# Moving the PSUM copies of the shift-filter gradient from VectorE to ScalarE

## The chip, the cores and the metric

The kernel runs on one core of a Trainium2 chip. The metric is the device time of one execution in microseconds (us). Of the kernel before there are three timed runs and one profiled execution, which is a run of its own with its own time. The engines are named as in the profile: PE is TensorE (matmuls and transposes, with PEld for its weight loads), DVE is VectorE, ACT is ScalarE, POOL is GpSimd, and SP is the engine that issues nearly all DMAs here (its issuing instructions are shown as SPq).

## The reference, cut to what matters

The forward pass adds two branches to its input x (2048 rows of 512): a gated long convolution and a gated bilinear layer. Both read xn, the layernorm of x. The reference returns the output and nine gradients for a given grad_out.

```python
k_shift = sum over t of k_pad[:, t:t+S, :] * shift_k[:, ks-1-t]     # ks = 4 taps per channel
kv = k_shift * v
y  = irfft(rfft(kv) * rfft(ssm_k))[:S] + kv * ssm_D                 # long causal convolution
out = x + xn * y + ((xn @ w_gate) * (xn @ w_up)) @ w_down
# outputs: out, then the gradients of q, k, v, shift_k, ssm_k, ssm_D, w_gate, w_up, w_down
```

Two small gradients matter for the change. The gradient of `shift_k` (512 channels, 4 taps) is, for each channel, the sum over the 2048 rows of the gradient of `k_shift` times `k` shifted by 0 to 3 rows. The gradient of `ssm_D` (512 numbers) is the gradient of the convolution's kernel at lag 0, as its product with `kv` is a sum over the same rows.

## The kernel before, in words

The 2048 rows lie as 128 partitions by 16 row groups (`R`). Early stages normalise x, run the bilinear layer forward and backward in chunks of rows (`ffn1`, `yb`), and do the convolutions as a two-step Fourier transform on PE (`g_fwd`, `g_mul`, `g_inv`). The change lies in the last stage, which fills the last 160 us or so of the span. Its spine is `dw` (from line 1046): for each of 11 blocks `fb` of 128 hidden units it runs `down_grad` (tile `pd`, 16 matmuls, gradient of `w_down`) and then the matmuls into `pu` (gradients of `w_gate` and `w_up`). For these the hidden activations must have the row dimension on partitions: blocks 0 to 6 are transposed on PE (`hid_t`, PSUM tile `pt`, copied by ACT into `nath` and `natd`). Blocks 7 to 10 (`TURNED`) come turned by a DMA (`load_t`, tile `natT`, line 817), except for the last chunk of rows, which `last_t` turns on PE (line 829) and ACT copies to an SBUF tile named `nat7` in the code and `nat` in the profile.

`dw` yields some six times for each block. At each yield the loop at the end of the kernel lets side jobs take a step: `inv_y`; `dsk_gram` from count 27 and then at every second count; `inv_dk` from 35 at every third (gradient of `ssm_k`; after its first part `put_dD` sends out the gradient of `ssm_D`); and `ew` from 10 at every third (elementwise work of DVE: `final` and `bwd`, whose results `put_late` sends out one step later).

`dsk_gram` handles 128 channels at a time (`c` from 0 to 3). For two halves of 64 channels, PE multiplies `dks` (64 channels by rows) by four shifted views of `k`, giving 64 x 256 products in PSUM (`pk`), of which only the diagonal of each 64 x 64 block is wanted. DVE multiplies by the identity (line 1091, tile `kd`) and sums (line 1093, `dsk`). After the four groups the sums are cast (`dskb`), turned by PE (`pts`, line 1101), copied by DVE (`dskt`) and sent out (line 1104). `put_dD` does the same with `dDs`, `ptd` and `dDt` (lines 1017 to 1020).

The order of each engine's instructions is laid down when the program is built. A planner takes the work in the order in which it is written, each engine taking the first that is ready by its own estimate; `tc.high_priority(offset=SOON)` counts its instructions as written 300 earlier, and `tc.issue_after` keeps a DMA's issue behind another. On the chip each engine then goes through its list in order. PSUM has three slots of two banks for tiles made by `P2` (`pk`, `pt`, `pu`, `po`, `pq`) and two of one bank for those made by `P1` (`pd`, `pts`, `ptd`). In SBUF the tag `dd` has two slots, shared by `dd` (from `inv_y`), `kd`, `nat7`, `dskt` and the last `og1`. A slot is free when the last reader of its tile is done; for `dskt` that is its outgoing DMA, for `nat7` the last matmul of its block.

The helpers `act` and `dve` (lines 235 and 238) are plain copies, so all copies of an engine carry one line number in the profile.

Of the kernel before, what the change touches and what calls it, by code (L numbers as in the profile page):

```python
# [9 lines left out]
F32 = mybir.dt.float32  # L10
I32 = mybir.dt.int32
ALU = mybir.AluOpType
ACTF = mybir.ActivationFunctionType
AX = mybir.AxisListType
# [7 lines left out]
P = 128  # L22
NC4 = 4
# [3 lines left out]
SOON = 300  # L27
# [163 lines left out]
def kernel(  # L191
# [24 lines left out]
    nc = tc.nc  # L216
# [17 lines left out]
    def act(o, i):  # L234
        nc.scalar.copy(o, i)  # L235

    def dve(o, i):
        nc.vector.tensor_copy(o, i)  # L238
# [13 lines left out]
    def P2(name, shape, dt=F32):  # L252
        return ps2.tile(shape, dt, name=name, tag="p2")

    def P1(name, shape, dt=F32):
        return ps1.tile(shape, dt, name=name, tag="p1")

    ident = const.tile([P, P], BF, name="ident")
# [658 lines left out]
    c2b = ctx.enter_context(tc.tile_pool(name="c2b", bufs=2, side="right", reuse_waits="tile"))  # L917
# [8 lines left out]
    dsk = c2.tile([P, NC4, 4], F32, name="dsk")  # L926
# [62 lines left out]
    def inv_dk():  # L989
        o5t = c2.tile([P, NC4, P, R], BF, name="o5t", tag="o5k")  # L990
        o5 = out_5.rearrange("(c q) s -> c q s", q=P)
        for rq in range(4):
            gk = gks.pop(0)
            if rq == 0:
                gk_last = load_gk_last()
            for b in range(2):
                po = P2("po", [P, 2, 4, P])
                for h in range(2):
                    for i in range(4):
                        for c in range(2):  # L1000
                            nc.tensor.matmul(po[:, h, i, :], lhsT=(gk_last(c, i) if rq == 3 else gk[:, c, i])[:, cs(2 * b + h)], rhs=TB.IW[:, c, :],
                                             start=(c == 0), stop=(c == 1))
                act(o5t[:, 2 * b:2 * b + 2, :, 4 * rq:4 * rq + 4], po[:].rearrange("q h r s -> q h s r"))
                if b == 1 and rq < 2:
                    gks.append(load_gk(2) if rq == 0 else None)
                if rq == 3:
                    for c in (2 * b, 2 * b + 1):
                        nc.sync.dma_start(o5[c], o5t[:, c].rearrange("q s r -> q (s r)"))
                yield
            if rq == 0:  # L1010
                yield from put_dD(o5t)

    def put_dD(o5t):
        act(dDs[:], o5t[:, :, 0, 0])
        yield
        pt = P1("ptd", [P, P], BF)
        nc.tensor.transpose(pt[:NC4, :], dDs[:], ident[:])
        dDt = c2.tile([NC4, P], BF, name="dDt")
        dve(dDt[:], pt[:NC4, :])
        nc.sync.dma_start(out_6.rearrange("(c p) -> c p", p=128), dDt[:])  # L1020

    def down_grad(fb):
# [56 lines left out]
    def dsk_gram():  # L1079
        for c in range(NC4):  # L1080
            pk = P2("pk", [P, 2, D])
            for r in range(R):
                for h in range(2):
                    c0 = c * 128 + 64 * h
                    nc.tensor.matmul(pk[64 * h:64 * h + 64, h, 0:256], lhsT=dks[:, r, c0:c0 + 64],
                                     rhs=KH[0][:, r:r + 4, c0:c0 + 64], start=(r == 0), stop=(r == R - 1))
            kd = c2b.tile([P, 4, 64], F32, name="kd", tag="dd")
            with tc.high_priority(offset=SOON):
                for h in range(2):
                    hs = slice(64 * h, 64 * h + 64)  # L1090
                    nc.vector.tensor_tensor(kd[hs], pk[hs, h, 0:256].rearrange("q (j c) -> q j c", j=4),
                                            ident[hs, hs].unsqueeze(1).to_broadcast((64, 4, 64)), op=ALU.mult)
                nc.vector.tensor_reduce(dsk[:, c, :], kd[:], axis=AX.X, op=ALU.add)
            yield
        dskb = c2.tile([P, 4, NC4], BF, name="dskb")
        nc.vector.tensor_copy(dskb[:], dsk[:].rearrange("q c i -> q i c"))
        for _ in range(2):
            yield
        pt = P1("pts", [P, 4, P], BF)
        for j in range(4):  # L1100
            nc.tensor.transpose(pt[:NC4, j, :], dskb[:, 3 - j, :], ident[:])
        dskt = c2b.tile([NC4, P, 4], BF, name="dskt", tag="dd")
        dve(dskt[:], pt[:NC4].rearrange("c j q -> c q j"))
        nc.sync.dma_start(out_4.rearrange("(c p) j -> c p j", p=128), dskt[:])
        yield

# [88 lines left out]
    def load_dk():  # L1195
        gks.append(load_gk(0))
        gks.append(load_gk(1))
        yield

    sides = [every(seq(inv_y(), load_dk()), 0, 3), every(dsk_gram(), 27, 2), every(inv_dk(), 35, 3), every(ew(), 10, 3)]  # L1200
    for n, _ in enumerate(dw()):
        for sd in sides:
# [36 lines left out]
```

## Time and profile before

| what | us |
|---|---|
| median of three runs (lowest to highest) | 480.83 (479.9 to 481.28) |
| the profiled execution, its own time | 481.82 |
| its span, first to last instruction | 480.0 |
| busy in the span: PE | 464.5 (97%) |
| busy in the span: DVE | 340.5 (71%) |
| busy in the span: ACT | 305.6 (64%) |
| 8 multiplies of line 1091 | 0.422 each (median) |
| 4 sums of line 1093 | 0.414 each (median) |
| copy `dskt` / copy `dDt` on DVE | 0.679 / 0.204 |

The times of a line in the timeline are its start and its length in us from the span's start. "idle before" is time in which the engine did nothing, with what ended it. The granted clock of TensorE was 0.999 on average. In the trace some records of matmuls are missing, so a group of 16 can be shown as 15.

### The profile page before, as it was taken

The page shows a single profiled execution, that of the slowest core. Times are in us where ns is not written, and L with a number is a line of the kernel's source. Part 1 is how long each engine was busy: PE and PEld are TensorE (multiplying, and loading weights), DVE is VectorE, ACT ScalarE, POOL GpSimd, SP SyncE. Part 2 cuts the span into 40 slices and gives each one's busy share as a digit, 9 for nine tenths or more (in the row PEclk, how much of TensorE's full clock was granted, in tenths as well). Part 3 has the DMA queues.
Part 4 walks back from the last instruction along what each step waited for, and adds up shares of the span by engine and source line. Part 5 has one row for each costly group of instructions (what it writes and reads, how often), then busy time and mean ns, then how long its engine had stood idle before and what let it go on. Part 6 is the DMA issues. An engine that isn't in the chain of part 4 may idle for free.

```text
span 480.0 us, 10366 instructions
## 1 busy us (share of the span) xinstructions
PE 464.5 (97%) x4252; PEld 311.6 (65%) x4293; DVE 340.5 (71%) x609; ACT 305.6 (64%) x349; POOL 14.0 (3%) x30
## 2 busy tenths in 40 slices
PE   7999999999999999999999999999999999999996
PEld 6867755547648447447447743576777687677885
DVE  7889989979366567686777877022257899599893
ACT  4957677659568678779779975375576535233141
POOL 8000000000000000000000000110000000000000
PEclk9999999999999999999999999999999999999999
DMA  8999999989998968968978379999899979999858
GB/s 268 374 381 366 310 296 320 315 300 328 318 288 270 277 202 255 285 200 245 298 235 259 118 272 331 388 329 313 312 361 364 371 260 320 318 267 239 252 155 294
DMA packets 111132, 139.85 MB, mean 291 GB/s; under 512 B 38859, under 2 KB 84336, under 8 KB 109550
## 3 DMA queue, kind: packets, MB, share of 16 engines
q1 hardware_dynamic: 109502, 137.85, 89.7%
q10 hardware_dynamic: 1584, 1.36, 1.0%
q8 instruction: 33, 0.54, 0.5%
q14 instruction: 13, 0.11, 0.1%
HBM read 67.08 MB, written 63.41 MB: 272 GB/s over the span
## 4 chain that ended last, share of the span: by engine, by line
PE 67%; DMA 15%; DVE 14%; issue 2%; SPq 2%; ACT 1%; DVEq 0%; ACTq 0%
PE px L555 15%; PE pgu L512 13%; PE pu L1062 8%; PE py L548 7%; PE pdh L518 6%; PE pd L1026 4%; PE ps L584 3%; DMA khC<-in_A_k_dram 3%; PE pg L613 3%; DMA ssk<-in_A_ssm_k_dram 2%; PE pf L370 2%; PE pt L859 2%; DMA vb<-in_A_v_dram 2%; DMA kb<-KS 2%; DMA x_b<-in_A_q_dram 2%
## 5 line engine op out<-in xcount | busy, mean ns | idle before, releaser
L555 PE MATMUL px<-WT,hd 128*128 128x512 bf16 (+1 forms) x340 | 78.6, 379 | 1.6 <-issue 1.4
L1062 PEld LDWEIGHTS <-xnC 128*128 128x128 bf16 x704 | 67.0, 98 | 8.4 <-issue 0.6
L555 PEld LDWEIGHTS <-hd 128*128 128x128 bf16 (+1 forms) x352 | 32.8, 98 | 44.4 <-issue 7.7
L235 ACT CAST gu<-pgu 128x1024 bf16<-128x1024 f32 (+1 forms) x48 | 45.4, 946 | 16.9 <-PE pgu L512 16.7
L235 ACT CAST GO<-pg 128x1024 bf16<-128x1024 f32 x48 | 46.2, 1015 | 13.8 <-issue 7.2
L235 ACT CAST SP<-ps 128x1024 bf16<-128x1024 f32 x47 | 45.5, 1025 | 13.7 <-PE ps L584 11.8
L512 PE MATMUL pgu<-xt,Wu 128*128 128x256 bf16 (+1 forms) x352 | 53.1, 273 | 1.1 <-DVE kn L238 0.6
L600 DVE TENSOR_TENSOR T<-SP 128x2048 bf16<-128x2048 bf16 x24 | 29.3, 1222 | 34.8 <-ACT SP L235 34.7
L512 PE MATMUL pgu<-xt,Wg 128*128 128x256 bf16 (+1 forms) x352 | 52.8, 273 | 0.0
L1062 PE MATMUL pu<-natd,xnC 128*128 128x256 bf16 x448 | 51.2, 273 | 0.0
L518 PE MATMUL pdh<-gt,WdT 128*128 128x256 bf16 (+1 forms) x352 | 46.9, 273 | 0.1
L235 ACT CAST fst<-pf 128x1024 bf16<-128x1024 f32 x44 | 42.7, 1031 | 5.5 <-issue 2.3
L512 PEld LDWEIGHTS <-Wu 128*128 128x128 bf16 (+1 forms) x352 | 33.0, 100 | 15.6 <-issue 10.7
L548 PE MATMUL py<-Wd,hd 128*128 128x512 bf16 (+1 forms) x167 | 40.2, 379 | 0.8 <-issue 0.5
L235 ACT CAST og<-pu 128x1024 bf16<-128x1024 f32 (+1 forms) x11 | 10.9, 993 | 43.7 <-PE pu L1062 28.3
L518 PEld LDWEIGHTS <-WdT 128*128 128x128 bf16 (+1 forms) x352 | 34.9, 100 | 4.8
L512 PEld LDWEIGHTS <-Wg 128*128 128x128 bf16 (+1 forms) x352 | 34.8, 100 | 3.7
L235 ACT COPY natd<-pt 128x2048 bf16<-128x2048 bf16 x14 | 26.2, 1875 | 12.0 <-PE pt L859 12.0
L533 DVE TENSOR_TENSOR hd<-gu,dh 128x1024 bf16<-128x1024 bf16 (+1 forms) x48 | 30.8, 641 | 0.8
L532 DVE TENSOR_TENSOR hd<-gu 128x512 bf16<-128x512 bf16 (+1 forms) x48 | 19.0, 397 | 16.7 <-ACT gu L235 16.7
L548 PEld LDWEIGHTS <-hd 128*128 128x128 bf16 (+1 forms) x176 | 16.5, 98 | 20.8 <-issue 3.1
L600 DVE TENSOR_TENSOR U<-SP 128x2048 bf16<-128x2048 bf16 x24 | 29.2, 1218 | 0.0
(177 smaller groups left out, 687.4 us busy)
## 6 DMA issues: line engine op xcount, KB each, us to landing
HDD<-hd SPq DMA_DIRECT2D x35, 384.0 KB, 4.5
FD<-fst SPq DMA_DIRECT2D x24, 512.0 KB, 4.9
X<-FD SPq DMA_DIRECT2D x24, 512.0 KB, 5.5
GD<-GO SPq DMA_DIRECT2D x24, 512.0 KB, 3.9
g<-GD SPq DMA_DIRECT2D x11, 1024.0 KB, 8.9
hb<-HDD SPq DMA_DIRECT2D x7, 1344.0 KB, 10.2
bb<-BX SPq DMA_DIRECT2D x8, 512.0 KB, 5.5
BX<-bx SPq DMA_DIRECT2D x7, 512.0 KB, 3.9
```

The lines of the kernel that those rows point to most:

```text
L235: nc.scalar.copy(o, i)
L512: nc.tensor.matmul(pgu[:w, i, t, :], lhsT=W[:, c, f0:f0 + w], rhs=xt[:, :, c, :], start=(c == 0), stop=(c == NC4 - 1))
L518: nc.tensor.matmul(pdh[:w, i, :], lhsT=WdT[:, c, f0:f0 + w], rhs=gt[:, :, c, :], start=(c == 0), stop=(c == NC4 - 1))
L532: nc.vector.tensor_tensor(hd[:fw, fb0:fb0 + n, 0, :], gu[:fw, :n, 0, :], gu[:fw, :n, 1, :], op=ALU.mult)
L533: nc.vector.tensor_tensor(hd[:fw, fb0:fb0 + n, 1:3, :], gu[:fw, :n], dh[:fw, :n].unsqueeze(2).to_broadcast((fw, n, 2, 256)), op=ALU.mult)
L548: nc.tensor.matmul(py[:], lhsT=hd[:fw, fb, 0, ss], rhs=Wd[:fw, fb, :], start=(fb == 0), stop=(fb == NFB - 1))
L555: nc.tensor.matmul(px[:], lhsT=hd[:fw, fb, t, ss], rhs=W[:fw, fb, :], start=(t == 1 and fb == 0), stop=(t == 2 and fb == NFB - 1))
L584: nc.tensor.matmul(ps[32 * q:32 * q + 32, a, :], lhsT=TB.EF[64 * a:64 * a + 64, 4 * g + q, ri].rearrange("p k j -> p (k j)"), rhs=X[64 * a ...
L600: tt(W[:].rearrange("p c a d -> p c (a d)"), A[:, i:i + 1].rearrange("p c a d -> p c (a d)").to_broadcast((P, 2, 2 * D)), B[:].rearrange(" ...
L613: nc.tensor.matmul(pg[q // 2][64 * a:64 * a + 64, q % 2, :], lhsT=TB.EI[32 * q:32 * q + 32, 2 * g + a, yi].rearrange("p k c -> p (k c)"), ...
L1026: nc.tensor.matmul(pd[:fw, :], lhsT=nat_h(fb, r), rhs=goC[:, r, :], start=(r == 0), stop=(r == R - 1))
L1062: nc.tensor.matmul(pu[:, c, :, :fw], lhsT=xnC[:, r, cs(c)], rhs=nat_d(fb, r), start=(r == 0), stop=(r == R - 1))
```

## The change

The eight multiplies no longer read PSUM. ACT copies each half of `pk` as float32 into `kd` in SBUF, and DVE multiplies there in place and sums. One `kd` tile of twice the size now serves two of the four groups, so that the four groups take two tiles of tag `dd` in place of four. The copies, multiplies and sums have no raised priority. The wait between `dskb` and the transposes into `pts` is four yields in place of two (the transposes are written at count 43 in place of 39). The copies `dskt` and `dDt` are made by ACT.

```diff
         dDt = c2.tile([NC4, P], BF, name="dDt")
-        dve(dDt[:], pt[:NC4, :])
+        act(dDt[:], pt[:NC4, :])
         nc.sync.dma_start(out_6.rearrange("(c p) -> c p", p=128), dDt[:])
...
-            kd = c2b.tile([P, 4, 64], F32, name="kd", tag="dd")
-            with tc.high_priority(offset=SOON):
-                for h in range(2):
-                    hs = slice(64 * h, 64 * h + 64)
-                    nc.vector.tensor_tensor(kd[hs], pk[hs, h, 0:256].rearrange("q (j c) -> q j c", j=4),
-                                            ident[hs, hs].unsqueeze(1).to_broadcast((64, 4, 64)), op=ALU.mult)
-                nc.vector.tensor_reduce(dsk[:, c, :], kd[:], axis=AX.X, op=ALU.add)
+            if c % 2 == 0:
+                kd = c2b.tile([P, 2, 4, 64], F32, name="kd", tag="dd")
+            for h in range(2):
+                hs = slice(64 * h, 64 * h + 64)
+                act(kd[hs, c % 2], pk[hs, h, 0:256].rearrange("q (j c) -> q j c", j=4))
+                nc.vector.tensor_tensor(kd[hs, c % 2], kd[hs, c % 2], ident[hs, hs].unsqueeze(1).to_broadcast((64, 4, 64)), op=ALU.mult)
+            nc.vector.tensor_reduce(dsk[:, c, :], kd[:, c % 2], axis=AX.X, op=ALU.add)
             yield
...
-        for _ in range(2):
+        for _ in range(4):
             yield
...
-        dve(dskt[:], pt[:NC4].rearrange("c j q -> c q j"))
+        act(dskt[:], pt[:NC4].rearrange("c j q -> c q j"))
         nc.sync.dma_start(out_4.rearrange("(c p) j -> c p j", p=128), dskt[:])
```

## The prediction

> **What bounds the kernel now.** I read the page first, for the busiest engine.
>
> ```profile
> span 480.0 us, 10366 instructions
> ...
> PE 464.5 (97%) x4252; PEld 311.6 (65%) x4293; DVE 340.5 (71%) x609; ACT 305.6 (64%) x349; POOL 14.0 (3%) x30
> ```
>
> PE leaves 15.5 us of the span unused, so this change can gain only what PE waits for the edited lines. The list of waits from 380 to 480 us (us in total, times, longest) says how much that is:
>
> ```profile
> ACT og L235 <- DMA out_dram<-og: 13.0, 2, 7.9
> ...
> PEld L859 <- DVE kd L1091: 1.9, 2, 1.5
> PE pt L859 <- DVE kd L1091: 1.3, 2, 1.1
> ```
>
> Two transposes wait until DVE has read `pk`, as they need its PSUM slot; ACT meanwhile idles long. The timeline of PE shows where (start, length):
>
> ```profile
> 401.47 0.28 PE L859 MATMUL pt<-ident,hd 128*128 128x128 bf16 x2
> 401.96 0.96 PE L859 MATMUL pt<-ident,hb 128*128 128x128 bf16 x14 [0.22 <-DVE kd L1091]
> ...
> 414.91 1.67 PE L1026 MATMUL pd<-goC,nath 128*128 128x512 bf16 x7
> 417.64 0.95 PE L859 MATMUL pt<-ident,hb 128*128 128x128 bf16 x14 [1.06 <-DVE kd L1091]
> ...
> 431.93 0.59 PE L1026 MATMUL pd<-goC,nat 128*128 128x512 bf16 x2
> 432.63 0.22 PE L1017 MATMUL ptd<-ident,dDs 128*4 128x128 bf16 x1
> 432.78 1.07 PE L1001 MATMUL po<-IW,g 128*128 128x128 bf16 x16
> ```
>
> The third place is not in the list of waits: `ptd` takes the slot of `pts`, which DVE empties from 431.90. Elsewhere after 389 PE is dense. Last the timeline of the other engines, for what runs beside PE to the end:
>
> ```profile
> 431.90 0.68 DVE L238 COPY dskt<-pts 4x512 bf16<-4x512 bf16 x1
> ...
> 432.61 0.29 SPq L1104 DMA_DIRECT2D out_dram<-dskt  x1
> ...
> 433.80 10.00 SPq L817 DMA_TRANSPOSE natT<-HDD  x2
> 443.91 0.53 SPq L1034 DMA_DIRECT2D out_dram<-od  x1
> ...
> 447.01 0.69 DVE L1138 TENSOR_TENSOR o<-xnC,yC 128x1024 bf16<-128x1024 bf16 x1 [1.68 <-DMA out_dram<-o]
> ...
> 467.10 0.33 SPq L1180 DMA_DIRECT2D out_dram<-dk  x1
> ...
> 476.73 0.34 SPq L1039 DMA_DIRECT2D out_dram<-od  x1
> ```
>
> SP stands in a turning DMA for 10 us; what is written behind it leaves from 443.91, `od` of block 7 first, though ACT had finished that at 433.15. A second chain follows: `o` goes out at 444.48, DVE gets the buffer at 447.01 and runs without a gap, SP waits for DVE's `dk` until 467.10 and then issues almost without pause to 476.32. The last `od` follows at 476.73. So PE's chain has only 0.41 us less room than SP's at the end.
>
> **The change part by part.**
>
> *PSUM slots of `pk`.* A copy of 64x256 float32 on ACT has no row; the nearest are `od` 96x256 (0.37) and `od` 128x512 (0.59). I take 0.37, as its 256 elements are the same, so 8 copies are 3.0 us of ACT; at most 4.7. Cover: `pk` number 3 ends at 410.30 and ACT idles from 405.47 to 414.00, so its slot is free at about 411.1, in place of 417.58. Number 1 ends at about 396.3, just when ACT starts `og` (396.31 to 397.32); its copies end at about 398.1, before the `natd` copy of 399.17 and before 401.6, when the slot is wanted. Number 0 ends at 390.9 with ACT idle, number 2 at 404.85, half a microsecond before ACT is free. Without that cover a copy would push ACT's next one back by 0.37 each. What PE gets: successive transposes normally follow after 0.11 (384.41 to 384.52), here after 0.49, so 0.38 us. From `pd`'s first half to the transposes is 1.73 (362.37 to 364.10); `pd` started at 414.69 (one record is missing; `po`'s 16 from 413.80 take 0.89), so they could start at 416.42 and not 417.64: 1.22 us. Together 1.60.
>
> One row speaks against ACT as the place, or for it: the copy of 512 elements took DVE 0.679 (`dskt`, 4 partitions) and ACT 0.588 (`od`, 128 partitions), so out of PSUM ACT is no slower here. [...]
>
> *DVE.* It loses `dskt` (0.68) and `dDt` (0.20). Eight multiplies from SBUF have no row; bounds are 0.422 as now and the 0.414 of a sum that reads 256 float32 from SBUF on one side, and twice the present price on the other, as the write in place is new: 8 x (-0.01 to +0.42), from -0.1 to +3.4 us. I take 0.422, the same elements. All lies before 447.01, where DVE waits 1.68 us for a DMA, and before 413.62, where it waits 4.29; that hides it. Without raised priority they come later on DVE, but nothing of PE waits for them until `pts`, now after 430. A multiply that waits for ACT holds all of DVE behind it (`final`, `bwd`): about 1.2 us for number 1 (copy done 398.1, not 396.9), covered by the same 4.29.
>
> *`pts` four counts later.* Its 0.32 us of PE (424.75 to 425.07) move behind `pd` of block 7. Net nothing, but the slots of P1 turn: `ptd` now needs the slot of that `pd`, which ACT's `od` copy (0.59) empties. On the old clock less 1.92 (1.60 and the moved 0.32), PE is free at 430.44, `pts` ends at 430.76, `od` at 431.23, then `ptd`, and `po` starts at 431.43 in place of 432.78: 1.35 gained. If `po` is put ahead of `ptd`, it starts at about 430.8 and the gain is 1.9. ACT's two new copies (0.59 and 0.20, from `od` 128x512 and `dDs`) lie in idle stretches of 0.74 and 2.81.
>
> *SP.* Now `dskt`'s DMA stands ahead of `dk`, `bb` and the turning pair, and SP waits 1.3 us there for DVE. Afterwards it is written behind the pair (count 43 against 42), so `dk` can go at 431.2 and not 432.95: up to 1.7 us sooner. But the pair moves data only when earlier transfers are through (`g`, 1 MB, went out at 430.65), so between 0 and 1.7; I take 0.9, the middle. On the other side `dskt`'s issue (0.35 with its gap) lands ahead of `o`. The chain over DVE and SP thus comes 0.55 earlier (bounds: 0.35 later to 1.35 earlier).
>
> *Sum.* PE gains 1.35 to 1.9, but the last `od` of SP can only come 0.41 + 0.55 = 0.96 earlier (0.06 to 1.76). I take 0.9 us. Against the profiled execution: 481.82 - 0.9 = 480.9. That execution stood 0.99 above the median of the runs, so there it is 480.83 - 0.9 = 479.9, with bounds 480.8 and 479.1.
>
> **The rivals.**
>
> *The tail comes along in full.* `dk`, `bb` and the pair move by the whole 1.7 and `po` goes ahead of `ptd`: 1.5 to 1.9 us, 479.1. For it: SP idles 1.3 us for `dskt` today. Against: the DMA engines are busy in that stretch.
>
> *Nothing comes through, or the new lists lose a little.* SP's tail keeps its place, or other orders of ACT and DVE give back the 1.6. With the tail kept: 480.8. With a new PE stall of the size of the old ones (1.2 to 1.5): up to 482.3.
>
> *`dskt` blocks the slot of `nat7` (slower).* Tag `dd` has two slots. When block 8's `nat7` is due (ACT, 437.71 today), one is held by block 7's until its last `pu` at 441.2, the other by `dskt` until its DMA has landed. Today that DMA leaves at 432.61. Behind the pair it leaves at about 444.5 less 0.9, and 2.3 us to landing (as `od`) gives 445.9. If the planner gave `nat7` that slot, ACT's list stands there until 445.9, the copy (0.80) ends at 446.7, and the last two matmuls of `pd` (444.92 today) come 1.8 late: 482.6, between 481.8 and 483.5 as the pair comes 1.7 or 0 earlier. If it took the other slot (free at about 439.5), nothing is lost. It decides when `dskt` lands later than about 443. For it: `od` of block 7 was ready at 433.15 and left at 443.91. Against: a planner that foresees the late DMA takes the other slot.
>
> **How the numbers follow.** A run of this kernel tells about 0.3% (1.44 us) from no change. Forecast 0.34, within 0.3%. Full tail 0.22, counted as faster. Blocked slot 0.36, of which 0.28 beyond +1.44 and 0.08 within. Lost in new lists 0.08, slower. So faster 0.22, same 0.42, slower 0.36. The predicted time is 479.9, with its own range 479.1 to 480.8. The range for 8 in 10 takes in most of the full tail and of the blocked slot: 478.9 to 483.2.
>
> **What would show it.** Right: no wait of L859 for L1091; transposes at about 401.6 and 416.1; `po` near 431.4; the pair on SP before 433.8 and `dskt` behind it. Wrong: a wait of ACT's `nat` copy for the DMA of `dskt` near 437, PE idle before the last two matmuls of `pd` near 444; or `og` and `natd` copies pushed back by those of `kd`.

## The result, and the profile after

| what | us |
|---|---|
| before, median of 22 runs (lowest to highest) | 480.16 (478.38 to 481.83) |
| after, median of 22 runs (lowest to highest) | 482.38 (479.81 to 485.06) |
| ratio after to before, with its 95% interval | 1.0049 (1.0033 to 1.0066) |
| the profiled execution of after: its own time, its span | 484.63, 482.8 |

The change makes the kernel slower by about 0.5%. The forecast was a gain of 0.9 us. The time is near the price of the third rival (482.6); how far that is luck is said below.

The page of the kernel after, its first lines:

```profile
span 482.8 us, 10377 instructions
...
PE 466.8 (97%) x4252; PEld 313.2 (65%) x4293; DVE 339.3 (70%) x607; ACT 309.0 (64%) x359; POOL 13.9 (3%) x30
```

The work moved as the diff says: DVE is busy 1.2 us less, ACT 3.4 us more. PE's matmuls are the same, and yet it is busy 2.3 us longer; 1.56 us of that is worked out below, from a lower clock. The list of waits from 380 to 490 us of the kernel after (us in total, times, longest):

```profile
ACT nat L235 <- DMA out_dram<-dskt: 12.0, 1, 12.0
...
PE pd L1026 <- ACT nat L235: 2.7, 1, 2.7
```

No transpose waits for `kd` any more. In its place there is one wait of 12 us, in which ACT's copy into `nat` (`nat7` of block 8) stands until the outgoing DMA of `dskt` has landed, and behind that copy PE idles 2.7 us. PE's timeline of the kernel after shows both (start, length):

```profile
402.53 0.28 PE L859 MATMUL pt<-ident,hd 128*128 128x128 bf16 x2
402.64 0.94 PE L859 MATMUL pt<-ident,hb 128*128 128x128 bf16 x14
...
415.58 1.67 PE L1026 MATMUL pd<-goC,nath 128*128 128x512 bf16 x7
417.09 0.94 PE L859 MATMUL pt<-ident,hb 128*128 128x128 bf16 x14
...
431.79 0.56 PE L1001 MATMUL po<-IW,g 128*128 128x128 bf16 x7
...
447.04 1.03 PE L1026 MATMUL pd<-goC,nat 128*128 128x512 bf16 x2 [2.69 <-ACT nat L235]
447.87 1.91 PE L1001 MATMUL po<-IW,g 128*128 128x128 bf16 x16
```

The transposes of 402.64 and 417.09 follow without a wait, as forecast. (Times count from the start of each span. `pk` number 3, with counting from 0, starts at 409.10 here and at 408.43 in the profile before, so times of the two profiles are compared with that 0.67 in mind.) But the last two matmuls of `pd` of block 8 wait 2.69 us, and the work after them is slow: `po`'s 16 matmuls run from 447.87 to the start of `pu` at 449.57, 1.70 us. In the profile before, ACT's copy waited for its transposes alone, PE had no gap there, and the same 16 took 0.89 to the next start. From its timelines of ACT and PE:

```profile
437.71 0.80 ACT L235 COPY nat<-pt 128x768 bf16<-128x768 bf16 x1 [2.81 <-PE pt L829]
...
444.92 0.59 PE L1026 MATMUL pd<-goC,nat 128*128 128x512 bf16 x2
445.35 1.06 PE L1001 MATMUL po<-IW,g 128*128 128x128 bf16 x16
```

The timeline of SP and ACT of the kernel after shows what the 12 us are:

```profile
431.29 0.35 SPq L1180 DMA_DIRECT2D out_dram<-dk  x1
...
432.16 10.82 SPq L817 DMA_TRANSPOSE natT<-HDD  x2
443.08 0.53 SPq L1034 DMA_DIRECT2D out_dram<-od  x1
443.71 0.29 SPq L1104 DMA_DIRECT2D out_dram<-dskt  x1
...
446.19 0.80 ACT L235 COPY nat<-pt 128x768 bf16<-128x768 bf16 x1 [12.03 <-DMA out_dram<-dskt]
```

`dskt` is ready in SBUF at 432.63. Its DMA is behind the turning pair on SP and leaves only at 443.71. The chain that ended last runs through this DMA (2.37 us), the `nat` copy (0.81) and the two matmuls of `pd`. The windows of the kernel after show why PE was slow behind the gap (stretch, length, busy time of PE, PEld, DVE, ACT and POOL with their instructions, granted clock, DMA share, GB/s):

```profile
444.00:447.00 3.00, 0.34 (x2) 0.00 (x0) 2.96 (x11) 0.81 (x2) 0.00 (x0) 0.98 1.15 362
447.00:450.00 3.00, 2.96 (x20) 2.29 (x21) 3.00 (x5) 2.49 (x4) 0.00 (x0) 0.50 0.97 279
```

Around the end of the gap TensorE's granted clock is 0.50 from 446.86 to 450.27, that is for 3.41 us; before and after it is 1.00.

### The profile page after: what moved, and what is told of

The parts are those of the page before. It is cut to its first block, busy times and chain, and to the rows that moved or that the text cites. A ratio compares the mean times of both kernels' runs of the same rounds, so it can differ in the third digit from the quotient of the medians.

```text
span 482.8 us, 10377 instructions
## 1 busy us (share of the span) xinstructions
PE 466.8 (97%) x4252; PEld 313.2 (65%) x4293; DVE 339.3 (70%) x607; ACT 309.0 (64%) x359; POOL 13.9 (3%) x30
## 4 chain that ended last, share of the span: by engine, by line
PE 70%; DMA 15%; DVE 8%; SPq 4%; issue 2%; ACT 1%; ACTq 0%; DVEq 0%
PE px L555 14%; PE pgu L512 13%; PE pu L1062 10%; PE py L548 7%; PE pdh L518 6%; PE pd L1026 5%; DMA hb<-HDD 5%; PE pt L859 3%; SPq L817 3%; PE ps L584 3%; PE pf L370 3%; PE pg L613 3%; DMA ssk<-in_A_ssm_k_dram 3%; PE pq L932 2%; DMA x_b<-in_A_q_dram 2%
## 5 line engine op out<-in xcount | busy, mean ns | idle before, releaser
L512 PEld LDWEIGHTS <-Wu 128*128 128x128 bf16 (+1 forms) x352 | 33.0, 100 | 15.1 <-issue 10.1
L235 ACT COPY natd<-pt 128x2048 bf16<-128x2048 bf16 x14 | 26.3, 1875 | 10.1 <-PE pt L859 10.1
```

The lines of the kernel that those rows point to most:

```text
L512: nc.tensor.matmul(pgu[:w, i, t, :], lhsT=W[:, c, f0:f0 + w], rhs=xt[:, :, c, :], start=(c == 0), stop=(c == NC4 - 1))
```

## The experiments

Theory S (slot): the whole loss comes from `dskt` holding a slot of tag `dd` until a DMA that now goes out behind the turning pair. Its rivals: the copies on ACT themselves cost the time (theory C), or it is only four yields in place of two, whatever the engine (theory Y, a part of S). Later, as the forecast gain had not shown up either, the question was what the copies are worth alone, and what the clock adds. The ratios are against runs of the kernel before on the same chip, with 95% intervals.

A yardstick that needs no whole-run time: the stretch from the start of `pk` number 3 to the start of the last two matmuls of the last `pd`. It holds everything the change touches after the first three `pk`, and its length is 65.41 or 65.42 us in all six profiles in which PE has no wait of the kinds discussed here.

### dskt in memory that nothing else waits for

```diff
-        dskt = c2b.tile([NC4, P, 4], BF, name="dskt", tag="dd")
+        dskt = hds[1][:NC4, 0, 0:2, :].rearrange("c t (a j) -> c (t a) j", j=4)
```

> The changed kernel with one edit: dskt lies in a part of the hidden-activation tile that is no longer used, so it takes no slot of tag dd. Theory (the slot of dskt blocks the copy of nat): ACT's nat copy of block 8 follows its transposes at once, as before the change, the 2.7 us gap of PE near 444 is gone, and what the freed PSUM slots gave (1.8 us at the first pu of block 7) stays, less what the tail over SP and DVE holds back: 0.5 to 1.8 us below the kernel before, that is 478.4 to 479.7 against 480.2, granted clock 0.999 or more in all runs. Rival (the extra copies on ACT or the new order of the lists cost the time): it stays above the kernel before, 481 to 483.

Measured: 479.43 us (12 runs) against 479.62; ratio 0.9996 (0.9983 to 1.0009). From the timelines of ACT, SP and PE (`dskt` is called `hd` here, after the tile in whose unused part it lies):

```profile
435.28 0.80 ACT L235 COPY nat<-pt 128x768 bf16<-128x768 bf16 x1 [2.81 <-PE pt L829]
...
441.27 0.29 SPq L1104 DMA_DIRECT2D out_dram<-hd  x1
...
442.49 0.59 PE L1026 MATMUL pd<-goC,nat 128*128 128x512 bf16 x2
```

The DMA of `dskt` still goes out late, at 441.27, but `nat` is copied at 435.28, as soon as its transposes are there, and PE has no gap. The yardstick is 65.42 (after: 69.82). All copies on ACT and all four yields are kept, so theory C falls and S stands. But the gain doesn't appear, neither the forecast one nor the 0.5 to 1.8 us expected here: this is what the change would be worth without its slot, and it can't be told from nothing.

### Two yields again

```diff
-        for _ in range(4):
+        for _ in range(2):
             yield
```

> The changed kernel with two yields in place of four before the transposes into pts. nat still takes the slot of dskt, but the DMA of dskt is written ahead of the turning pair. Theory (the lateness of that DMA is the cost): it leaves SP near 432, ACT's nat copy is not held, and the time is 0 to 1.6 us below the kernel before (478.6 to 480.2). Rival (copies on ACT cost the time, the yields don't matter): 481 to 483.

Measured: 478.90 (12 runs) against 479.62; ratio 0.9981 (0.9966 to 0.9997). Repeated on another chip:

> The version with two yields once more, to see whether its lead of 0.19% over the kernel before (interval 0.03 to 0.34%) is real. From the two later profiles of the kernel before, in which PE loses nothing to kd, PE has nothing to gain in the usual run: ratio 0.998 to 1.000, and from pk number 3 to the last two matmuls of pd again 65.4 us. If the lead is real by another way: 0.998 again with an interval that leaves out 1.

Measured: 478.98 (12 runs) against 479.97; ratio 0.9986 (0.9974 to 0.9999). `dskt`'s DMA leaves at 431.12, ahead of the pair; `nat` still waits for it, but gets the slot at 436.75 while PE is busy, and the yardstick is 65.42 and 65.41. The copies on ACT with the old place of the transposes are slightly faster than before, by 0.14 to 0.19%, with intervals that barely leave out no change. Where that would come from isn't shown: the yardstick is the same as in two later profiles of the kernel before (below).

### Four yields in the kernel before

```diff
-        for _ in range(2):
+        for _ in range(4):
             yield
```

> The kernel before with one edit: four yields in place of two. No copy is moved to ACT. Theory: the DMA of dskt falls behind the turning pair here too, nat waits for it, PE stands before the last two matmuls of block 8's pd: 481.5 to 484 against 480.2, and the wait of nat for the DMA of dskt is in the list of waits. As the two waits of PE for kd are still there, PE arrives later and the gap should be 1 to 2 us shorter than the 2.7 of the changed kernel. Rival (copies on ACT): 480.2, no such wait.

Measured: 480.80 (12 runs) against 479.62; ratio 1.0027 (1.0011 to 1.0042). That is slower, but by less than the expected 481.5 to 484, and the two waits for `kd`, expected to be still there, were not in this execution. From its timelines of SP, ACT and PE:

```profile
441.56 0.29 SPq L1104 DMA_DIRECT2D out_dram<-dskt  x1
...
443.90 0.80 ACT L235 COPY nat<-pt 128x768 bf16<-128x768 bf16 x1 [10.29 <-DMA out_dram<-dskt]
444.76 0.61 PE L1026 MATMUL pd<-goC,nat 128*128 128x512 bf16 x2 [0.95 <-ACT nat L235]
```

With every copy still on VectorE the same wait appears. It is the four yields that put `dskt` behind the pair. The gap is 0.95 us in this execution because the pair took 9.32 here and `dskt` left at 441.56; counted from `pk` number 3 that is 1.61 earlier than in the first profile of after, and the gap is 1.74 shorter. One of the 12 runs, the longest (483.16), has a mean clock of 0.995, the others 0.999 or 1.0.

### Work for PE in the gap

```diff
         for r in range(R):
+            if fb == 8 and r == R - 2:
+                warm(ident, 44)
             nc.tensor.matmul(pd[:fw, :], lhsT=nat_h(fb, r), rhs=goC[:, r, :], start=(r == 0), stop=(r == R - 1))
```

This is the kernel after with 44 transposes of the identity, used by nothing, ahead of the two matmuls that wait.

> The changed kernel with 44 extra transposes of the identity (0.055 us each, some 2.4 us, result unused) put on PE just ahead of the two matmuls that wait for nat, to fill the gap with work. The wait of ACT for the DMA of dskt stays. Theory (the gap also lowers the granted clock for some 3 us after it): clock 0.999 or more in all runs, po after the gap takes 0.9 and not 1.7 us, and the time is that of the runs of the changed kernel whose clock stayed at 0.999 (median 480.9, and up to 481.5 if the filling runs over). Rival (the clock drops for another reason, or the drop costs nothing): clock 0.996 in about half of the runs and 482 to 484.

Measured: 482.11 (6 runs) against 479.62; ratio 1.0056 (1.0034 to 1.0079). PE's timeline of this kernel:

```profile
442.95 2.62 PE L481 MATMUL warm<-ident 128*128 128x128 bf16 x44
445.49 0.60 PE L1028 MATMUL pd<-goC,nat 128*128 128x512 bf16 x2
445.93 1.06 PE L1001 MATMUL po<-IW,g 128*128 128x128 bf16 x16
```

The transposes last as long as the gap, and ACT's `nat` copy still waits its 11.7 us. The two `pd` matmuls take 0.44 us to the next start and not 0.83, and the clock stays at 1.00. The time can't tell what that saves, which the expectation overlooked: the 44 transposes cost 2.54 us themselves, and 479.43 without the blocked slot plus 2.54 is 482.0. So the same with 20:

> The changed kernel with 20 extra transposes of the identity (1.1 us) ahead of the two matmuls that wait for nat, in place of the 44 (2.5 us) that by themselves take as long as the gap. Theory (without the work the gap is long enough in about half of the runs to halve the granted clock for 3 us, which costs 1.5 us more): the clock stays at 0.999 or more in nearly all runs, and the time is the gap alone, 480.5 to 482, with few runs or none above 482.5. Rival (it is the wait alone, the clock costs nothing): spread and median as in the changed kernel, 479.8 to 485, median 482.4.

Two of its 12 executions took 539 us (mean clock 0.852) and 1237 us; they are left out, and with them the profile, which is of the second. In the other ten the mean clock is 0.999 or more, so with these 20 in the gap (some 1.15 us, an estimate from the 2.54 of the 44) the clock stayed up as well. They lie between 479.65 and 482.51, with a median of 481.36 against 480.14; ratio 1.0023 (1.0002 to 1.0044). None reaches 484, as seven of the 22 runs of after do.

### The kernel after, once more

> The changed kernel a second time, for its profile alone. Theory: nat's copy again waits some 10 to 12 us for the DMA of dskt, and PE stands before the last two matmuls of block 8's pd; the gap is 1 to 3 us as the turning pair ends sooner or later. If it is under some 2 us, the granted clock stays at 1.0 after it and the time is 480 to 481.5; if above, the clock shows 0.5 for some 3 us after it and the time is 482 or more.

Measured: 481.67, with a gap of 2.47 us in place of 2.69. The expected divide at some 2 us is not borne out: the gap is longer, and the clock stays. One window of this execution, after the gap that ends at 445.63:

```profile
446.00:449.00 3.00, 3.00 (x37) 2.73 (x35) 2.18 (x4) 2.81 (x4) 0.00 (x0) 1.00 0.87 282
```

The same kernel, and no drop of the clock: 37 matmuls in 3 us where the first profile had 20 (its window begins with the two longer ones of `pd`; in the 3 us from the end of each gap it is 34 and 21). The yardstick is 68.05, that is 65.42 + 2.63, nearly all of it the gap. The first profile of after had 69.82. Its further 1.77 us are 0.22 of longer gap and 1.56 of half clock (0.40 in the two `pd`, 0.81 in `po`, 0.35 in the first pass of `pu`). The 22 runs fall into two groups by their mean clock: 12 at 0.995 or 0.996, as in the first profile, with a median of 484.13, and 10 at 0.999 or 1.0, with a median of 480.94.

### The kernel before, twice more

> The kernel before once more, unchanged, for a second profile and as a measure of how far two measurements of one kernel differ. Theory (the waits of PE for kd in the first profile were partly chance, as they hang on when a DMA lets DVE go on near 409 to 417): from the start of pk number 3 to the start of the last two matmuls of pd it takes less than the 66.82 us of the first profile, down to 65.4 plus the moved transposes, and the wait of the transposes near 417 for kd is shorter than 1.06 or gone. Rival (PE always loses 1.6 us to these waits, and what the changed lists gain is taken back in the tail): 66.8 again and both waits. Ratio within 0.2% of 1.

Measured: 480.13 (12 runs) against 480.14, ratio 1.0003 (0.9984 to 1.0023). Its profiled execution took 479.76. From the timelines of SP and PE:

```profile
399.62 7.54 SPq L817 DMA_TRANSPOSE natT<-HDD  x1
...
414.88 1.89 PE L1026 MATMUL pd<-goC,nath 128*128 128x512 bf16 x8
416.60 0.94 PE L859 MATMUL pt<-ident,hb 128*128 128x128 bf16 x14
```

Here is the place where the prediction read 1.06 us of waiting for `kd`. This execution of the same kernel has none, there or anywhere, and the yardstick is 65.41 (66.82 in the profile that the prediction read). Once more:

> The kernel before a third time, for its profile alone. As for the second: theory, the two waits of PE for kd differ from profile to profile (0 to 1.3 us in all); rival, they are 1.3 us every time.

It took 480.59, and has no wait for `kd` either; yardstick 65.41. What differs is SP: the turning DMA of block 7 took 9.69 us in the first profile and ended 0.31 after the start of `pk` number 3; in the later two it took 7.54 and 7.81 and ended 1.45 and 1.18 before that start. What SP issues behind it, DVE's inputs among it, comes later by as much (`o` goes out 0.36 after that start in the first, 1.41 and 1.14 before it in the later two), so DVE reaches `kd` later. Two more kernels that keep the old copies of `pk` fit: with four yields alone (above) that DMA ended 1.16 before that start and there is no wait for `kd`, and with only the two small copies moved (below) it ended 0.28 before and the wait is 0.57. The link is still argued from five profiles, not tested: nothing was run that changes the length of that DMA alone. It doesn't cover the shorter wait of 0.22 at 401.96, which comes before that DMA ends.

### Only the copies of pk, and only the two small ones

The kernel after with two yields and with `dskt` and `dDt` copied by VectorE:

```diff
-        act(dDt[:], pt[:NC4, :])
+        dve(dDt[:], pt[:NC4, :])
...
-        act(dskt[:], pt[:NC4].rearrange("c j q -> c q j"))
+        dve(dskt[:], pt[:NC4].rearrange("c j q -> c q j"))
```

> The kernel before with only the copies of pk on ACT (and one kd tile for two groups): dskt and dDt by DVE and two yields, as before. If these copies free the PSUM slots and cost nothing else: no wait of L859 for kd, and 0 to 1.3 us below the kernel before (478.3 to 479.6 against 479.6), the larger part of what the version with two yields gained (0.9). If copies on ACT cost time: 480 or more.

Measured: 480.02 (12 runs) against 480.14; ratio 0.9993 (0.9977 to 1.0009). It keeps a wait that the two small copies on ACT avoid; PE's timeline of this kernel:

```profile
433.05 0.22 PE L1017 MATMUL ptd<-ident,dDs 128*4 128x128 bf16 x1 [1.06 <-DVE dskt L238]
```

In this execution SP's turning DMA ended late (0.2 after the start of `pk` number 3), and no transpose waited for `kd`. So the copies do what the prediction said of them, where there is something to remove. The other half, the kernel before with only these two copies on ACT:

```diff
-        dve(dDt[:], pt[:NC4, :])
+        act(dDt[:], pt[:NC4, :])
...
-        dve(dskt[:], pt[:NC4].rearrange("c j q -> c q j"))
+        act(dskt[:], pt[:NC4].rearrange("c j q -> c q j"))
```

> The kernel before with only dskt and dDt copied by ACT (two yields, Gram's sums as before). Nothing of PE's waits for these two in the usual run; the slot of pts may come free up to 0.4 us sooner for ptd. Theory: no measurable change, ratio 0.998 to 1.001. Rival (small copies on ACT hold back the copies that PE needs): 1.002 or more.

Measured: 479.31 (12 runs) against 479.97; ratio 0.9987 (0.9975 to 1.0000). Its profile has one wait for `kd`, 0.57 us, and none for `dskt`. Either half is worth at most 0.25%, and the intervals don't tell the halves apart.

### dskt's DMA from ACT's queue

The kernel after, all four yields kept, with the one DMA issued by ACT and so not behind the pair:

```diff
-        nc.sync.dma_start(out_4.rearrange("(c p) j -> c p j", p=128), dskt[:])
+        nc.scalar.dma_start(out_4.rearrange("(c p) j -> c p j", p=128), dskt[:])
```

> The changed kernel with one edit: the DMA of dskt is issued by ACT, right behind its own copy, and not by SP. Four yields and the shared slot stay. Theory (what costs is that this one small DMA stands behind the turning pair on SP): it leaves at about 433, lands at about 435.5, nat's copy follows near its old place (437), PE has no gap at the last two matmuls of block 8's pd: 479 to 480.2, like the version with its own slot (479.4 against 479.6). Rival (slot sharing as such, or four yields): 481 to 483.

Measured: 479.09 (12 runs) against 479.97; ratio 0.9983 (0.9968 to 0.9997). From the timelines of ACT and SP:

```profile
431.84 10.58 SPq L817 DMA_TRANSPOSE natT<-HDD  x2
432.31 0.53 ACTq L1104 DMA_DIRECT2D out_dram<-dskt  x1
...
437.36 0.80 ACT L235 COPY nat<-pt 128x768 bf16<-128x768 bf16 x1 [3.46 <-DMA out_dram<-dskt]
```

The slot is the same, the wait of `nat` is for the same DMA, and it ends at 437.36 in place of 446.19, early enough for PE. The position behind the pair is therefore the cause. With that mended the change is at most a small gain: 0.17% here, and 0.04%, which can't be told from nothing, with the slot of its own.

## Why the prediction was wrong, step by step

**What failed: the choice of the likeliest case.** The prediction had the mechanism and the place as a rival at 0.36, a chance above the 0.34 of the case that it forecast: `dskt` landing at 445.9 (measured 446.09) and the `nat` copy done at 446.7 (446.99). It named what would decide, a landing later than about 443. That its 482.6 is so near the measured 482.38 is partly luck: it was counted from a median of 480.83, which is 480.16 over 22 runs, it held no cost of the clock, and the runs after stand in two groups, at 480.94 and 484.13. What it left open was which of the two slots the planner would give to `nat7`. It gave the one of `dskt`; the argument against, that a planner sees the late DMA coming, was not worth what was put on it. The kernel before gave a hint, since `dskt` shares a tag with a tile that is on PE's path and its release depends on a queue.

**What failed: "PE gets 1.60".** The 0.38 and 1.22 us were real in the profile that was read, and the changed kernel's profiles don't have them: from `pk` number 3 on, behind the 0.38, the profiles without a gap are 1.40 us shorter (65.42 for 66.82). But they stood in one execution of 481.82, which is 1.7 above the later median of 480.16, and two more profiles of the same kernel have none. The prediction noticed that the execution stood 0.99 above the median of three, and carried the whole gain across to the median all the same. The forecast of 479.9 had its 0.9 from waits that the usual run lacks. What two yields or the ACT queue leave, 0.7 to 0.9 us, is about as much, but it isn't shown to come from these waits, and so the agreement with the forecast 0.9 is luck. Five of the 12 times of the unchanged kernel in the first repeat lie at 481.5 to 482.4 and seven at 479.1 to 480.2, so an execution with such waits may be an ordinary one in its upper group; since not every execution has a profile, this stays open. There is another source: in the five profiles of kernels with the old copies, `pk` number 3 starts between 407.24 and 409.50, so the work ahead of the yardstick alone differs by 2.3 us.

**What was missing: the price of a gap of PE beyond its length.** The rival priced the stall at 1.8 us, as lateness against the profile before. PE's gap is 2.47 to 2.69, as PE reached it at 444.35 and not 444.92 while `nat` came 0.3 later, and the half clock costs 1.56 us more in the first profile. The mean clock of 12 of the 22 runs is as low as there. For those runs the sum closes: 2.69 + 1.56 = 4.25 against 4.16 measured (484.13 less 480.16, plus the 0.19 by which the kernel with its own slot is below before). For the other ten it doesn't: their median lies 0.97 above the same base, less than the gap of 2.47 that the second profiled execution without the drop shows, and that one took 481.67, more than any of the ten. How long the gap was in them isn't known; 0.95 in the experiment with four yields alone shows that it can be short.

**The tail.** "So PE's chain has only 0.41 us less room than SP's at the end" was also of that one execution. From the yardstick's end to the end of the span it has 4.75 us. The later ones have 3.9, but for 4.0 in the kernel with only the copies of `pk` moved and 4.5 in the one with ACT's queue. The tail doesn't grow where the yardstick is short: it is 3.88 behind the 65.42 of the kernel with its own slot and 3.90 behind the 66.54 of the one with four yields alone. So it is not what kept the forecast gain back. The 15.5 us that PE was read to leave unused are of that trace too, in which 41 of 4293 matmul records are missing; a later one of the same kernel that has them all leaves 477.9 less 467.8, or 10.1.

**What held.** The size of each moved operation. The tile view of the kernel after (times of one: least, median, most, in ns):

```profile
L235 ACT COPY kd<-pk x8: 366/367/372, 392.1 to 411.5; 64x256 f32<-64x256 f32 x8
L1092 DVE TENSOR_TENSOR kd<-kd,ident x8: 408/416/423, 396.2 to 417.9; 64x256 f32<-64x256 f32 x8
```

0.367 where 0.37 was taken, and 0.416 where 0.422 was taken, with the double price as the upper bound that didn't come. The copies `dskt` and `dDt` take 0.57 and 0.26 (taken: 0.59 and 0.20). All of it is hidden where the prediction hid it: the kernel with `dskt` in memory of its own keeps all of it and is no slower than before. The multiply from SBUF is only 0.006 us shorter than from PSUM here. Out of PSUM ACT was no slower: the copy into `dskt` took ACT 0.57 and DVE 0.68. ACT's 0.367 beside DVE's 0.416 points the same way, though a float32 copy and a multiply of two sources are not the same work.

`po` went ahead of `ptd`, with 7 of its 16 matmuls, the better of the two cases given. The pair went out 1.6 us earlier and ended 0.8 earlier (443.0 for 443.8), against 0.9 taken; counted from `pk` number 3 it is 2.3 and 1.5. That the pair moves data only when earlier transfers are through fits the DMA rates of the profile before: behind the turning DMA of block 7, issued at 399.05, they are 393 GB/s until 404, 22 from 405.0 to 405.8 and 293 from 406 to 409; behind the pair, issued at 433.80, they are 388 from 437 to 438, 9 from 439.3 to 439.9 and 305 from 440 to 441. No run tests it by itself.

## What to carry to other kernels

A tile that is sent out holds its slot until its DMA has landed (here ACT's `nat` copy stood 12.03 us for the one of `dskt`), so where that DMA stands in its queue belongs to the price of moving it. Before a small output is moved later, list what is ahead of it in that queue (here a turning pair of 10 us) and what else takes slots of its tag; a slot of its own or another queue took the late wait away here. And a wait seen in one profile is one sample: before a gain is counted from it, look at whether that execution stands above the median by about as much, and at a second profile.

## What the runs showed of the hardware

A gap of PE of 2.69 us was followed by 3.41 us at a granted clock of 0.50, from 0.18 before its end on, which cost 1.56 us; a gap of 2.47 in the same kernel was followed by a clock of 1.00, and with 20 transposes that nothing uses in the gap the mean clock was 0.999 or more in all of the ten runs that count. So of these two executions one paid for its gap about the length alone, the other over half as much again. What decides between the two is not shown.

A turning DMA of the same size held SP for 7.54 to 9.69 us in three executions of the kernel before, and the pair for 8.53 to 10.82 over all profiles. What is issued behind it on SP moves with it: with a pair of 9.32 `dskt` left at 441.56 and PE's gap was 0.95, with one of 10.82 it left at 443.71 and the gap was 2.69.
